# Chunked attention with a router behind it: the triangle inverse in 16-wide blocks and three rounds of products, the state's decay on VectorE, transfers and preparation in written order

## The chip, the cores and the metric

The kernel runs on one core of a Trainium2 chip. The metric is device time in microseconds (us), from the start to the end of one execution. Engines are named as in the profile: PE (TensorE), DVE (VectorE), ACT (ScalarE), POOL (GpSimd), SP (SyncE, which only issues transfers here).

## The reference

An attention with a state of 40 x 40 for each of 4 x 8 heads runs over 768 steps; its output, as 3072 rows of 320, goes through a mixture of 8 experts, two for each row.

```
for t in range(S):
    y[:, :, t] = np.einsum('bhd,bhde->bhe', rt, state)
    Sa = np.einsum('bhde,bhe->bhd', state, at)
    state_decay = state * wt[:, :, None, :] - np.einsum('bhd,bhe->bhde', Sa, bt)
    state = state_decay + np.einsum('bhd,bhe->bhde', vt, kt)
...
logits = x @ w_gate
noisy_logits = logits + np.log1p(np.exp(x @ w_noise)) * noise
# the two largest of 8 per row, softmax over the two
out[mask] += top2_w[mask, k, None] * (np.maximum(x[mask] @ w1[e], 0.0) @ w2[e])
```

## The kernel before

The 768 steps are done in chunks of 64. Within a chunk the recurrence is a triangular system, so that the kernel inverts a unit lower triangular 64 x 64 matrix for each head and does the rest with products. Two halves of the batch alternate (p = 0, 1), and two chunks (c = 0, 1) make a group g of 6: the work is a chain of 24 **units**, n = 4g + 2c + p, each one chunk of one half with 16 heads. The state `Sst[p]` goes from unit n to unit n + 2.

A unit issues on PE, in this order: `pkb` (UY<-P,kbt: the output of the unit before), `state` (pd and WS<-Sst,A), `rows` of the unit before (pg), `umm` (WS<-w,dT and UY<-dT,w: the product with the inverse), `akv` of the next unit (WS<-Vz,ak), `zmm` (UY<-dd,lo), `sumin` (WS<-Sst,idf: copies the state into the accumulator), `spmm` (WS<-vu,kbt), `dmm` (pD<-dd,Z), `rnmm`, `rmm`, and preparation for a later group: transposes (`quad`, ptr<-idf,KB) and scores (`score`, sc<-A,KB). ACT and DVE copy and scale between these; the first of it is ACT's copy w<-WS, which ends `state`. I count a unit from one such copy to the next.

Preparation of a group, per half: loads (raww, A, KB), a scan and `newton` on DVE, logarithm and exponential on ACT, the products `mula` and `mulk` (A<-A,Gx and KB<-KB,NH, 104x1024) on POOL, then scores. `prepS` copies the scores to `lt` and `lo` on ACT, and `lt` and the like go to DRAM (`scr`), from where `Solve` takes them as X, 128 lines of a 32 x 32 block. `Solve.step` makes the inverse of the 32-wide diagonal blocks in 30 pairs of multiply and add on X and Tt (30 to 240 elements a line); the table `SLV` says which pairs go to POOL and which to DVE, and in which slot of which unit. `done` writes X to DRAM, has ACT transpose it (Xn), and writes that. `fetchB` reads both back in 10 transfers for each unit (dd, dT), and `zmm` and `dmm` make the corner that joins the two 32-wide blocks of a chunk.

The class `Eng` (L397) makes each instruction on PE, DVE, ACT and POOL follow the one written before it on the same engine, and each waits there for its data. SP's order is left to the scheduler. The slots ('ld', 'p0', 'f1', 'p1', 'f2', 'f3', 'a1', 'qa', 'a2', 'qb', 'sc') are places in a unit's code where preparation is put by `ev`.

The router is `logits` for each unit (lg<-pg on DVE) and `route` after units 7, 15, 19, 21 and 23 (8, 8, 4, 2 and 2 tiles of 128 rows), which runs whole inside `finish` of the next unit: two dozen small instructions on DVE and ACT, products on PE (pr<-cnt,tri), then positions. `scatter` sends 4 indirect transfers a unit, or all that are left (ls<-ent, one for 128 entries, on POOL). The weights of the first expert (w1r, w2r) are loaded and split in two 16-bit parts by ACT and DVE (w1h, w1l, w2h, w2l) as soon as the scheduler places them, which is while the last units run. After unit 24's `finish` the eight experts run, to the end.

Of the kernel before, what the change touches and what calls it, by code (L numbers as in the profile page):

```python
# [17 lines left out]
R=104  # L18
# [27 lines left out]
class Moe:  # L46
    def __init__(s,nc,tc,ctx,aps):
        s.nc,s.tc=nc,tc
        s.wgn_d,s.nz_d,s.w1_d,s.w2_d,s.out_d=aps
        ec=ctx.enter_context  # L50
        s.kp=ec(tc.tile_pool(name="mk",bufs=1))
        s.rp=ec(tc.tile_pool(name="mr",bufs=MRB))
        s.dp=ec(tc.tile_pool(name="md",bufs=1,space=DRAM))
        s.scat=[]; s.half=0; s.parts=PARTS; s.cap=CAP; s.rts=list(RTS); s.todo=[]
        s.consts()
# [48 lines left out]
    def logits(s,n,xt,pl,ps,tag):  # L104
# [18 lines left out]
    def route(s,n0,T,ps,tag,bufs):  # L123
# [29 lines left out]
        if n0+T>=NA: s.scatter(len(s.todo))  # L153
    def scatter(s,n,after=()):
# [9 lines left out]
    def gate(s,lg,nzt,T,w0,w1):  # L164
# [249 lines left out]
class Solve:  # L414
    def __init__(s,a,g,scr):
        s.a,s.g,s.j,s.l=a,g,0,{}
        s.X=a.tmp.tile([128,32,32],F32,name="X"); s.T=a.tmp.tile([128,240],F32,name="Tt")
        s.fl=s.X.rearrange("p a b->p (a b)")
        s.xd=a.nc.sync.dma_start(s.fl,scr.rearrange("k p b x n->(k p b x) n"))
    def step(s,eng,n=1):  # L420
        X,T=s.X,s.T
        for _ in range(n):
            j=s.j; s.j+=1
            if j>30: return
            if j==0:
                s.a.nc.gpsimd.affine_select(out=X,in_=X,pattern=[[-1,32],[1,32]],base=0,channel_multiplier=0,compare_op=ALU.is_gt,fill=0.0)
                s.a.nc.gpsimd.memset(s.fl[:,0:1024:33],1.0)
            else:
                m=31-j; t=T[:,:j*m].rearrange("p (k i)->p k i",i=m)
                eng.tensor_tensor(t,X[:,j:j+1,j+1:].to_broadcast([128,j,m]),X[:,0:j,j:j+1].to_broadcast([128,j,m]),op=ALU.mult)  # L430
                s.l=eng.tensor_tensor(X[:,0:j,j+1:],X[:,0:j,j+1:],t,op=ALU.add)
    def done(s,eng):
        nc,a=s.a.nc,s.a
        s.step(eng,31)
        scr2=a.dr.tile([2,2,2,CG*8,1024],F32,name="scr2"); scr3=a.dr.tile([2,2,CG*8,1024],F32,name="scr3")
        nc.sync.dma_start(scr2.rearrange("k p b x n->(k p b x) n"),s.fl)
        Xn=a.inp.tile([64,32,32],F32,name="Xn",bufs=1)
        nc.scalar.activation(Xn,s.X[0:64].rearrange("p j t->p t j"),AF.Copy)
        nc.sync.dma_start(scr3.rearrange("p b x n->(p b x) n"),Xn.rearrange("p a b->p (a b)"))
        return scr2,scr3  # L440

class Att:
    def __init__(s,nc,tc,ctx,aps):
        s.nc,s.tc,s.aps=nc,tc,aps
        ec=ctx.enter_context
        s.inp=ec(tc.tile_pool(name="inp",bufs=1))
        s.tmp=ec(tc.tile_pool(name="tmp",bufs=1))
        o=sorted(range(SAB),key=lambda i:(i-2*NG)%SAB); s.sab={i:ec(tc.tile_pool(name=f"sab{i}",bufs=1)) for i in o}
        s.stk=ec(tc.tile_pool(name="stk",bufs=1))
# [8 lines left out]
        s.Z=s.UY[:,:,256:384].rearrange("p b (i t)->p b i t",t=32)  # L458
        s.consts()
    def consts(s):  # L460
# [4 lines left out]
        s.KB=[t([128,NS,2,64],F32,name=f"KB{i}") for i in range(2)]  # L465
        s.A=[t([128,NS,64],F32,name=f"A{i}") for i in range(SAB)]
# [10 lines left out]
        s.dT=[t([128,2,4,64],F32,name=f"dT{i}") for i in range(2)]  # L477
        s.Z2=t([128,2,4,64],F32,name="Z2")
# [13 lines left out]
    def burst(s,f):  # L492
        for g in f: i=g()
        return i
# [43 lines left out]
    def prepS(s,G,scr):  # L538
        nc=s.nc; sp,p=G['sp'],G['p']
        lt=s.tmp.tile([128,CG*2*4*32],F32,name="lt"); lo=sp.tile([128,32+CG*2*4*32],F32,name="lo")  # L540
        nc.gpsimd.memset(lo[:,0:32],0.0)
        G['lo']=lo; v=lambda z: z.rearrange("p (c q i t)->p c q i t",c=CG,q=2,i=4)
        pp=s.score(G,1)
        for z,t0 in ((lt,0),(lo[:,32:],32)): s.act(v(z).rearrange("p c q i t->p q c i t"),pp[:,:,:,t0:t0+32].rearrange("p q (c i) t->p q c i t",c=CG))
        for i in range(4):
            b,k=divmod(i,2)
            s.sl=nc.sync.dma_start(scr[k,p,b].rearrange("x (j t)->j x t",j=32),(lt,lo[:,32:])[k][32*i:32*i+32].rearrange("p (x t)->p x t",t=32))
    def prepK(s,G):
        ak=G['ak']=s.stk.tile([128,2,CG*4,64],F32,name="ak",bufs=AKB)
# [15 lines left out]
    def fetchA(s,o):  # L565
        nc=s.nc; p,cc=o['p'],o['cc']
        vu=o['vu']=s.stk.tile([128,2,2,4,40],F32,name="vu",bufs=VB)
        nc.sync.dma_start(vu[0:64].rearrange("p b q i e->p b (q i e)"),s.aps[1][p,cc].rearrange("(b s) x->s b x",b=2))
        rv=s.RV[o['n']%2]; nc.sync.dma_start(rv[0:R].rearrange("p x h t->p (x h t)"),s.aps[2][p,cc])
        o['r'],o['v']=rv[:,0],rv[:,1]  # L570
    def fetchB(s,o,S2):
        nc=s.nc; c,p=o['c'],o['p']; scr2,scr3=S2
        d=o['dT']=s.dT[o['n']%2]; dd=o['dd']=s.stk.tile([128,2,4,32],F32,name="dd",bufs=2)
        f=lambda z,q: z.rearrange("(c q i) (j t)->c q j i t",c=CG,q=2,j=32)[c,q]
        for b in range(2): nc.sync.dma_start(dd[64*b:64*b+32].rearrange("p q i t->p (q i) t"),scr3[p,b].rearrange("(c x) (j t)->c j x t",c=CG,j=32)[c])
        for q in range(2):
# [324 lines left out]
```

## Time and profile before

| | us |
|---|---|
| time, median of 3 runs | 1067.43 (1060.68 to 1069.38) |
| the profiled execution's own time | 1061.36 |
| its span in the trace | 1059.7 |
| up to the first unit's copy w<-WS | 93.4 |
| the 24 units, first to last such copy | 529.8 |
| last unit, last route, gather, experts | 436.5 |

The span is what the trace covers; 1.7 us of the execution lie outside it. In a row of the trace's timeline stand start, duration, engine, line, operation, output<-inputs with shape, how many instructions are merged, and in brackets the engine's idle time before them with the instruction that ended it ("issue" is none that the profile shows). Line 403 is the ordering wrapper, through which most instructions pass, so that they are told apart by tile names.

### The profile page before, as it was taken

How to read it: one execution, taken by the hardware profiler on the slowest of the kernel's cores; microseconds unless marked ns; L12 is line 12 of the kernel's file. 1: busy time of each engine (PE TensorE's matmuls, PEld its weight loads, DVE VectorE, ACT ScalarE, POOL GpSimd, SP SyncE). 2: the span in 40 equal slices, each digit the busy share in tenths (PEclk: the TensorE clock that was granted, in tenths of full speed). 3: DMA queues.
4: the chain of work that ended last, by engine and by line, in shares of the span. 5: the costliest groups of instructions: out<-in, count | busy, mean ns of one | idle time of the engine just before them, and what ended most of it. 6: DMA issues, size and time to landing. Idle time of an engine off the chain costs nothing. (4 is left out here: it accounts for less than half of the span.)

```text
span 1059.7 us, 29111 instructions
## 1 busy us (share of the span) xinstructions
PE 778.2 (73%) x12693; PEld 585.9 (55%) x12693; DVE 505.8 (48%) x1030; ACT 323.6 (31%) x654; POOL 370.8 (35%) x430
## 2 busy tenths in 40 slices
PE   1226555488658888668476661899999999999995
PEld 1114444477547777547365551475756666675663
DVE  8186364345446365513422207347556566555231
ACT  2024313133314234202221212245354434434231
POOL 8026330542464362352003101534334352531403
PEclk9967967659859789956665755899999999999998
DMA  8654733445637554512833523335434362621303
GB/s 193 162 96 91 157 77 85 102 103 140 134 83 148 136 129 120 138 23 76 231 112 93 139 58 124 82 58 166 92 100 99 94 156 53 173 25 17 38 10 38
DMA packets 187294, 110.00 MB, mean 104 GB/s; under 512 B 144818, under 2 KB 175414, under 8 KB 187078
## 3 DMA queue, kind: packets, MB, share of 16 engines
q1 hardware_dynamic: 174997, 90.90, 34.7%
q0 software_dynamic: 12160, 17.15, 9.2%
q8 instruction: 102, 1.67, 0.7%
q14 instruction: 35, 0.28, 0.1%
HBM read 81.73 MB, written 29.67 MB: 105 GB/s over the span
## 5 line engine op out<-in xcount | busy, mean ns | idle before, releaser
L303 POOL DMA_INDIRECT out_dram<-y,le x48 | 79.9, 1665 | 198.0 <-ACT y L297 196.4
L282 DVE SCALAR_TENSOR_TENSOR hl<-ph,hh 128x320 f16<-128x320 f32 (+1 forms) x128 | 74.1, 589 | 77.0 <-ACT hh L281 74.3
L281 ACT ACTIVATE hh<-ph 128x320 f16<-128x320 f32 (+1 forms) x128 | 65.9, 517 | 131.1 <-PE ph L280 109.9
L280 PEld LDWEIGHTS <-w1h 128*128 128x128 f16 x768 | 74.9, 99 | 54.7 <-issue 2.7
L294 PEld LDWEIGHTS <-hh 128*128 128x128 f16 (+1 forms) x1024 | 84.3, 101 | 35.0 <-issue 2.9
L403 PE MATMUL sc<-A,KB 64*64 64x64 f32 x1536 | 40.1, 275 | 79.6 <-ACT lo L403 21.6
L403 PEld LDWEIGHTS sc<-A,KB 64*64 64x64 f32 x1536 | 36.2, 184 | 85.0 <-issue 33.3
L403 POOL TENSOR_TENSOR KB<-KB,NH 104x1024 f32<-104x1024 f32 x20 | 51.0, 2570 | 69.0 <-PE pD L403 21.0
L294 PE MATMUL po<-w2h,hh 128*128 128x320 f16 (+1 forms) x512 | 73.2, 284 | 0.0
L403 DVE TENSOR_TENSOR Tt<-X 128x234 f32<-128x234 f32 (+14 forms) x128 | 52.5, 410 | 42.9 <-POOL X L403 39.7
L249 POOL DMA_INDIRECT xr<-xd,le x56 | 53.2, 950 | 50.9 <-issue 41.5
L294 PE MATMUL po<-w2h,hl 128*128 128x320 f16 (+1 forms) x512 | 68.6, 283 | 0.0
L294 PE MATMUL po<-w2l,hh 128*128 128x320 f16 (+1 forms) x512 | 67.9, 282 | 0.0
L280 PE MATMUL ph<-xh,w1h 128*128 128x512 f16 (+1 forms) x256 | 67.5, 347 | 0.5 <-DVE hl L282 0.5
L280 PE MATMUL ph<-xl,w1h 128*128 128x512 f16 (+1 forms) x256 | 66.5, 341 | 0.0
L280 PE MATMUL ph<-xh,w1l 128*128 128x512 f16 (+1 forms) x256 | 66.4, 341 | 0.0
L403 PE MATMUL UY<-P,kbt 128*64 128x64 f32 x768 | 36.7, 262 | 34.3 <-DVE P L403 29.2
L403 DVE TENSOR_TENSOR P<-sc,mk 128x512 f32<-128x512 f32 x48 | 30.8, 684 | 50.7 <-PE sc L403 50.7
L403 POOL DMA_INDIRECT ls<-ent,po x48 | 48.8, 1016 | 17.4 <-issue 12.2
L297 ACT ACTIVATE y<-po,le 128x320 f32<-128x320 f32 (+1 forms) x56 | 28.3, 505 | 84.6 <-PE po L294 84.5
L403 PEld LDWEIGHTS UY<-P,kbt 128*64 128x64 f32 x768 | 32.5, 172 | 37.6 <-DVE P L403 30.6
L403 PE MATMUL pD<-dd,Z 32*64 32x32 f32 x768 | 37.6, 245 | 20.9 <-ACT Z L403 12.1
(214 smaller groups left out, 1613.0 us busy)
## 6 DMA issues: line engine op xcount, KB each, us to landing
w2r<-in_w_dram SPq DMA_DIRECT2D x8, 1280.0 KB
KB<-in_fm_dram SPq DMA_DIRECT2D x24, 416.0 KB
RV<-in_rv_dram SPq DMA_DIRECT2D x24, 416.0 KB
w1r<-in_w_dram SPq DMA_DIRECT2D x8, 1024.0 KB
raww<-in_fm_dram SPq DMA_DIRECT2D x12, 422.5 KB
A<-in_fm_dram SPq DMA_DIRECT2D x12, 416.0 KB
w1r<-in_w_dram SPq DMA_DIRECT2D x16, 256.0 KB
vu<-in_vt_dram SPq DMA_DIRECT2D x24, 160.0 KB
```

The lines of the kernel that those rows point to most:

```text
L249: for k in range(c,c+a): nc.gpsimd.indirect_dma_start(out=x[:p,k],out_offset=None,in_=s.xd[w],in_offset=OFFS(ap=li[:p,k,0:1],axis=0))
L280: for i,(a,b) in enumerate(mm): nc.tensor.matmul(ph[:,:n],a,b,start=i==0,stop=i==7)
L281: nc.scalar.activation(hh[:,f],ph[:,:n],AF.Relu)
L282: nc.vector.scalar_tensor_tensor(hl[:,f],ph[:,:n],0.0,hh[:,f],op0=ALU.max,op1=ALU.subtract)
L294: for j in range(c): nc.tensor.matmul(po[p*j:p*j+p,:d],h[:,f,r],w[:,f,d*j:d*j+d],start=k==0,stop=k==23)
L297: nc.scalar.activation(y[:,:d],po[:,:d],AF.Copy,scale=w_[:,ii:ii+1])
L303: st=nc.gpsimd.indirect_dma_start(out=o_,out_offset=OFFS(ap=ix,axis=0),in_=yv,in_offset=None,compute_op=ALU.add)
L403: i=f(*a,**kw)
```

## The change

- **Inverse**: `Solve` works on 16-wide diagonal blocks, two for each line of 32, in 14 pairs of 28 to 112 elements. Pairs of all groups but the first are on POOL, in slot f1 of unit 4g-3, and `done` is in slot f2 of unit 4g-2. The first group's are on DVE, ahead of the units.
- **Products**: with N the score matrix without its diagonal blocks and D the block inverses, `mm1` forms M = DN and its transpose, `mm2` forms G = I + M² and H (with D), and `mm3` forms GH, which is added to D; `zmm` and `dmm` go. DVE adds the identities and D, ACT copies MT and H. D and its transpose are fetched into XD (every second unit, both halves) and XDT (each unit), each a single buffer.
- **State**: `sumin` goes; DVE adds `Sp` to `Sst` and multiplies by `ge`, in two instructions where there was one.
- **Order**: after the first part SP is put in written order too. The transfers scr<-lt are kept back in `late` and issued at the next unit's start (`flush`). Each unit but the last five now has the same kind of preparation, two quads and one score.
- **Router**: `route` is a generator that moves one step at each of six calls of `adv()` in a unit; `acc` moves from POOL to DVE.
- Tiles are fixed (`own`), no more taken from pools.

```diff
 class Solve:
     def step(s,eng,n=1):
-            if j>30: return
+            if j>14: return
...
-                m=31-j; t=T[:,:j*m].rearrange("p (k i)->p k i",i=m)
-                eng.tensor_tensor(t,X[:,j:j+1,j+1:].to_broadcast([128,j,m]),X[:,0:j,j:j+1].to_broadcast([128,j,m]),op=ALU.mult)
-                s.l=eng.tensor_tensor(X[:,0:j,j+1:],X[:,0:j,j+1:],t,op=ALU.add)
+                m=15-j; sh=[128,2,j,m]; t=s.T[:,:2*j*m].rearrange("p (a k i)->p a k i",a=2,i=m)
+                eng.tensor_tensor(t,V[:,:,j:j+1,j+1:].to_broadcast(sh),V[:,:,0:j,j:j+1].to_broadcast(sh),op=ALU.mult)
+                s.l=eng.tensor_tensor(V[:,:,0:j,j+1:],V[:,:,0:j,j+1:],t,op=ALU.add)
     def done(s,eng):
-        Xn=a.inp.tile([64,32,32],F32,name="Xn",bufs=1)
-        nc.scalar.activation(Xn,s.X[0:64].rearrange("p j t->p t j"),AF.Copy)
+        nc.scalar.activation(a.Xn,s.fl.rearrange("p (j t)->p t j",t=32),AF.Copy)
...
-    def fetchB(s,o,S2):
+    def fetchD(s,o,S2):
         for q in range(2):
+            for k in range(2): s.nc.sync.dma_start(s.XD[64*q+32*k:64*q+32*k+32].rearrange("p i b u t->p (i b u) t")[:,:,32*k:32*k+32],S2[0][k,o['c'],q].rearrange("i b p (j t)->j (i b p) t",j=32))
+    def fetchT(s,o,S2):
+        for b in range(2):
+            for k in range(2): s.nc.sync.dma_start(s.XDT[64*b+32*k:64*b+32*k+32,:,32*k:32*k+32],S2[1][k,o['c']][:,:,b,o['p']].rearrange("q i (t j)->t (q i) j",t=32))
...
+    def mm1(s,o,G):
+        for z in range(2):
+            for h,b in QB():
+                q,i=h%2,h//2; r=slice(64*b,64*b+64); x=D[r,4*q+i],N[r,q,4*c+i]
+                s.mm(pp[64*q:64*q+64,b,z,i],x[z],x[1-z],start=True,stop=True)
+        s.nc.vector.tensor_tensor(s.M1,pp[:,:,0],s.Ir.rearrange("p (o u) t->p o u t",u=1).to_broadcast([128,2,4,64]),op=ALU.add)
+        s.act(s.MT,pp[:,:,1])
...
-    def sumin(s,o): s.mm(s.Sp,s.idf,s.Sst[o['p']][...,0:40],start=True,stop=False)
...
-        s.nc.vector.tensor_tensor(s.Sst[o['p']][0:R,:,:,0:40],s.Sp[0:R],o['ge'].to_broadcast([R,4,2,40]),op=ALU.mult)
+        S=s.Sst[o['p']][0:R,:,:,0:40]
+        s.nc.vector.tensor_tensor(S,s.Sp[0:R],S,op=ALU.add); s.nc.vector.tensor_tensor(S,S,o['ge'].to_broadcast([R,4,2,40]),op=ALU.mult)
...
         for n in range(N+1):
-            if n<N: do(n,'ld'); fV(n+2)
+            s.flush(); do(n,'ld'); fV(n+2); do(n,'ld2')
             if r: s.pkb(r,Gof(n-1))
...
+            if x: s.mm1(x,Gof(n+1))
+            adv()
             if r: finish(r,n-1)
-            do(n,'f1')
+            adv()
             s.umm(o)
...
-            if n!=2: fB(n+2)
-            if n+1<N: s.akv(O[n+1],Gof(n+1)); s.zmm(O[n+1],Gof(n+1))
-            if not last: s.sumin(o); s.spmm(o,G)
+            if x: s.mm2(x); s.akv(x,Gof(n+1))
+            adv()
+            if not last: s.spmm(o,G)
+            fA(n+2)
             do(n,'f2')
-            if n+1<N: s.dmm(O[n+1])
-            if not first: s.rnmm(o)
             s.rmm(o)
-            fA(n+2)
-            do(n,'f3')
+            adv()
+            if x: s.mm3(x); fT(n+2); fD(n+2)
             do(n,'a1'); do(n,'qa',"pA"); do(n,'a2'); do(n,'qb',"pB"); do(n,'sc')
+            adv()
+            if not first: s.rnmm(o)
+            fR(n+2)
```

**First place: DVE in unit 3.** Numbers behind a name tell the buffers of one name apart. Before, the pairs of group 2's inverse (Tt, X) stand between the state (Sst) and the mask P, which `pkb` needs:

```order
L403 TENSOR_TENSOR Sst_138<-WS,ge 104x8x40
L403 TENSOR_TENSOR Tt<-X 128x130
L403 TENSOR_TENSOR X<-X,Tt 128x5x26
L403 TENSOR_TENSOR Tt<-X 128x150
L403 TENSOR_TENSOR X<-X,Tt 128x6x25
L403 TENSOR_TENSOR P<-sc,mk 128x512 x2
```

Of the change, from one scan (Gx, ge) to the unit's last instruction there, No:

```order
L422 SCALAR_TENSOR_TENSOR Gx_173<-raww_73,d_246 104x1024
L422 TENSOR_TENSOR ge_193<-Gx_173,raww_73 104x16
L422 TENSOR_TENSOR Ms<-sc,Ir 128x512
L422 TENSOR_REDUCE lg<-pg 128x16
L422 TENSOR_TENSOR Gs<-sc,Ir 128x512
L422 TENSOR_TENSOR Sst_263<-WS,Sst_263 104x8x40
L422 TENSOR_TENSOR Sst_263<-Sst_263,ge_197 104x8x40
L422 TENSOR_TENSOR P<-sc,mk 128x512 x2
L422 TENSOR_TENSOR dT<-UY,XD 128x512
L422 TENSOR_TENSOR No_105<-sc,mB 128x1024
```

The pairs that waited for POOL's have left DVE; Ms, Gs, dT, the second Sst and No have come.

**Second place: PE in unit 8, where the first route falls.** Before, pr stands right behind pg, ahead of `umm`:

```order
L403 MATMUL ptr<-idf,KB_117 128x128 x8
L403 MATMUL sc<-A_119,KB_117 64x64 x32
L403 MATMUL UY<-P,kbt 64x64 x16
L403 MATMUL pd<-idf,Sst_137 128x128 x4
L403 MATMUL WS<-Sst_137,A_122 64x40 x16
L403 MATMUL pg<-IW,yT 128x120 x4
L403 LDWEIGHTS tri
L403 MATMUL pr<-cnt,tri 128x64
```

Of the change, from `pkb` to `spmm`, where a whole unit's new order is seen:

```order
L422 MATMUL UY<-P,kbt_213 64x64 x16
L422 MATMUL pd<-idf,Sst_263 128x128 x4
L422 MATMUL WS<-Sst_263,A_165 64x40 x16
L422 MATMUL sc<-No_105,XDT 64x64 x16
L422 MATMUL sc<-XDT,No_105 64x64 x16
L422 MATMUL pg<-IW,yT 128x120 x4
L422 MATMUL WS<-w_274,dT 64x40 x16
L422 MATMUL UY<-dT,w_274 64x64 x16
L422 MATMUL sc<-MT,Ms 64x64 x16
L422 MATMUL sc<-XD,MT 64x64 x16
L422 MATMUL WS<-Vz_266,ak_125 64x80 x8
L422 MATMUL WS<-vu_270,kbt_217 40x40 x16
```

and, further on in the same unit, behind `rmm`:

```order
L422 MATMUL UY<-Hs,Gs 64x64 x16
L422 MATMUL ptr<-idf,KB_101 128x128 x8
L422 MATMUL sc<-A_169,KB_97 64x64 x32
L422 LDWEIGHTS tri
L422 MATMUL pr<-cnt,tri 128x64
```

`mm1` stands between `state` and pg, `mm2` between `umm` and `akv`, and pr has moved to the unit's end, behind the score.

**Third place: DVE in units 18 and 19, where the first two experts' weights come.** Before, expert 0's split stands in unit 18 between lg and P:

```order
L403 TENSOR_REDUCE lg<-pg 128x16
L205 TENSOR_REDUCE mx<-w1r 128x1
L223 SCALAR_TENSOR_TENSOR w1l<-w1r,w1h 128x1024 x2
L224 SCALAR_TENSOR_TENSOR w1h<-w1r,w1h 64x1024
L208 TENSOR_REDUCE yc<-w1l 128x1
L403 TENSOR_TENSOR Sst_137<-WS,ge 104x8x40
L208 TENSOR_REDUCE yc<-w1h 64x1
L205 TENSOR_REDUCE mx<-w2r 128x1
L233 SCALAR_TENSOR_TENSOR w2l<-w2r,w2h 128x640 x4
L205 TENSOR_REDUCE mx<-w1r 128x1
L403 TENSOR_TENSOR P<-sc,mk 128x512 x2
```

Of the change, from unit 18's last copies to unit 19's Gs (ak is group 5's):

```order
L224 TENSOR_REDUCE mx<-w2r 128x1
L242 SCALAR_TENSOR_TENSOR w1l<-w1r,w1h 128x1024 x2
L243 SCALAR_TENSOR_TENSOR w1h<-w1r,w1h 64x1024
L252 SCALAR_TENSOR_TENSOR w2l<-w2r,w2h 128x640
L227 TENSOR_REDUCE yc<-w1l 128x1
L252 SCALAR_TENSOR_TENSOR w2l<-w2r,w2h 128x640 x2
L422 TENSOR_TENSOR yT<-UY,Gx_185 104x2x4x64
L227 TENSOR_REDUCE yc<-w1h 64x1
L252 SCALAR_TENSOR_TENSOR w2l<-w2r,w2h 128x640
L224 TENSOR_REDUCE mx<-w1r 128x1
L422 TENSOR_TENSOR Ms<-sc,Ir 128x512
L422 TENSOR_REDUCE lg<-pg 128x16
```

The split now lies across the border of the two units, ahead of yT, and the second expert's first instruction (mx<-w1r) ahead of Ms; its mx<-w2r is the next row, ahead of Gs.

## Rows read from the trace of the kernel before

**Rows 1.** The page's first part, one engine: busy time, share of the span, instructions.

```profile
PE 778.2 (73%) x12693; PEld 585.9 (55%) x12693; DVE 505.8 (48%) x1030; ACT 323.6 (31%) x654; POOL 370.8 (35%) x430
```

**Rows 2.** Busy time by stretch, cut at the copies w<-WS of units 0, 5, 8, 16, 20 and 23. [...]

```profile
0.00:93.40 93.40, 23.42 (x440) 17.61 (x440) 56.96 (x99) 19.68 (x31) 37.74 (x82) 0.86 0.64 138
93.40:235.40 142.00, 86.40 (x2219) 74.08 (x2219) 69.56 (x112) 36.99 (x79) 52.70 (x62) 0.72 0.48 107
235.40:286.80 51.40, 40.08 (x1267) 35.01 (x1268) 26.62 (x56) 17.80 (x40) 17.02 (x24) 0.93 0.58 133
286.80:441.30 154.50, 121.46 (x3386) 104.85 (x3386) 80.00 (x187) 49.43 (x111) 74.49 (x92) 0.83 0.53 121
441.30:551.40 110.10, 68.50 (x1418) 58.65 (x1418) 36.19 (x104) 22.97 (x50) 22.47 (x33) 0.63 0.43 117
551.40:623.20 71.80, 45.96 (x1025) 39.63 (x1025) 17.33 (x82) 12.21 (x35) 13.29 (x20) 0.64 0.36 97
```

**Rows 3.** The same view of unit 14 alone.

```profile
411.50:426.50 15.00, 12.70 (x424) 11.17 (x423) 5.11 (x13) 6.10 (x12) 2.19 (x4) 1.00 0.45 121
```

**Rows 4.** The timeline of PE in unit 14, the rows of `akv`, `zmm`, `sumin`, `dmm`, the quads and the score.

```profile
415.50 0.77 PE L403 MATMUL WS<-Vz,ak 128*64 128x80 f32 x16 [1.82 <-ACT vu L403]
416.20 0.67 PE L403 MATMUL UY<-dd,lo 32*64 32x32 f32 x32
416.80 0.81 PE L403 MATMUL WS<-Sst,idf 128*128 128x320 f32 x2
...
418.27 1.12 PE L403 MATMUL pD<-dd,Z 32*64 32x32 f32 x32
...
420.88 1.09 PE L403 MATMUL ptr<-idf,KB 128*128 128x128 f32 x8
422.46 1.16 PE L403 MATMUL sc<-A,KB 64*64 64x64 f32 x64 [0.48 <-DVE Tt L403]
```

**Rows 5.** The timeline of DVE in unit 14, the state and the mask P.

```profile
418.46 0.49 DVE L403 TENSOR_TENSOR Sst<-WS,ge 104x320 f32<-104x320 f32 x1 [3.66 <-PE WS L403]
421.02 1.29 DVE L403 TENSOR_TENSOR P<-sc,mk 128x512 f32<-128x512 f32 x2 [2.07 <-PE sc L403]
```

**Rows 6.** The timeline ahead of the units: first and last DVE instruction of the first group's inverse, and ACT's first w<-WS.

```profile
54.25 0.19 DVE L403 TENSOR_TENSOR Tt<-X 128x30 f32<-128x30 f32 x1 [1.51 <-POOL X L403]
...
76.03 0.21 DVE L403 TENSOR_TENSOR X<-X,Tt 128x30 f32<-128x30 f32 x1
...
93.43 0.45 ACT L403 ACTIVATE w<-WS 128x320 f32<-128x320 f32 x1
```

**Rows 7.** The timeline of units 2 and 3: what waited for an inverse.

```profile
167.13 1.96 ACT L403 ACTIVATE Xn<-X 64x1024 f32<-64x1024 f32 x1 [13.53 <-DVE X L403]
...
169.72 1.54 PE L403 MATMUL ptr<-idf,KB 128*128 128x128 f32 x6 [11.87 <-ACT kbt L403]
...
200.25 1.01 PE L403 MATMUL UY<-P,kbt 128*64 128x64 f32 x14 [11.73 <-DVE P L403]
```

**Rows 8.** The costliest groups of POOL's instructions, shapes apart: count | busy us, mean ns | idle time before them.

```profile
L403 POOL TENSOR_TENSOR KB<-KB,NH 104x1024 f32<-104x1024 f32 x20 | 51.0, 2570 | 69.0 <-PE pD L403 21.0 <-PE UY L403 19.7 <-DMA KB<-in_fm_dram 17.4
...
L403 POOL TENSOR_SCALAR_AFFINE_SELECT X<-X 128x1024 f32<-128x1024 f32 x6 | 7.6, 1262 | 101.0 <-DMA X<-scr 56.1 <-DMA KB<-in_fm_dram 32.9 <-ACT dT L403 12.1
...
L403 POOL TENSOR_TENSOR X<-X,Tt 128x108 f32<-128x108 f32 x5 | 2.0, 393 | 0.4
...
L403 POOL TENSOR_TENSOR X<-X,Tt 128x30 f32<-128x30 f32 x2 | 0.5, 236 | 0.2
```

**Rows 9.** The timeline of unit 14: SP's issue of a group's load of X, and the first POOL instruction on it.

```profile
416.88 0.34 SPq L419 DMA_DIRECT2D X<-scr  x1
...
420.59 1.27 POOL L403 TENSOR_SCALAR_AFFINE_SELECT X<-X 128x1024 f32<-128x1024 f32 x1 [12.74 <-DMA X<-scr]
```

**Rows 10.** The timeline of PE at the route in unit 8.

```profile
295.90 0.21 PE L403 MATMUL pr<-cnt,tri 128*128 128x64 f16 x1 [8.06 <-DVE cnt L403]
```

**Rows 11.** Unit 16's scatters: the first and the last of 13 in POOL's timeline, and a stretch of 6 us within them (columns as in the second group).

```profile
453.22 1.02 POOL L403 DMA_INDIRECT ls<-ent,po  x1 [0.49 <-DVE po L403]
...
468.44 0.96 POOL L403 DMA_INDIRECT ls<-ent,po  x1 [0.30 <-issue]
...
459.00:465.00 6.00, 2.07 (x17) 1.57 (x17) 0.00 (x0) 0.38 (x1) 4.47 (x6) 0.50 0.03 2
```

**Rows 12.** The timeline of unit 18: the first expert's weights on ACT, SP's issue of w2r, and PE.

```profile
513.04 2.00 ACT L222 ACTIVATE w1h<-w1r 128x1024 f16<-128x1024 f32 x2 [8.69 <-DMA w1r<-in_w_dram]
...
514.15 0.40 SPq L216 DMA_DIRECT2D w2r<-in_w_dram  x1
...
516.72 1.92 PE L403 MATMUL pD<-dd,Z 32*64 32x32 f32 x32 [10.17 <-ACT Z L403]
...
520.85 2.62 ACT L232 ACTIVATE w2h<-w2r 128x640 f16<-128x640 f32 x4 [4.18 <-DMA w2r<-in_w_dram]
```

**Rows 13.** The timeline of unit 1: one POOL product and the DVE instructions beside and behind it.

```profile
134.33 2.34 POOL L403 TENSOR_TENSOR A<-A,Gx 104x1024 f32<-104x1024 f32 x1
134.40 2.47 DVE L403 TENSOR_TENSOR Tt<-X 128x184 f32<-128x184 f32 x1 [12.60 <-POOL X L403]
136.91 0.35 DVE L403 TENSOR_TENSOR X<-X,Tt 128x184 f32<-128x184 f32 x1
```

More of the change, by code (lines that the diff above doesn't have):

```diff
@@ L53, in __init__ @@
         s.dp=ec(tc.tile_pool(name="md",bufs=1,space=DRAM))
[L54 removed]
+        s.scat=[]; s.steps=[]; s.half=0; s.parts=PARTS; s.cap=CAP; s.rts=list(RTS); s.todo=[]
         s.consts()
@@ L122, in turn, with advance, route @@
         s.half=1
-    def route(s,n0,T,ps,tag,bufs):
+    def advance(s,all=False):
+        while s.steps:
+            if next(s.steps[0],None) is None: s.steps.pop(0)
+            elif not all: return
+            if not all: return
+    def route(s,n0,T,lg,ps,tag,bufs):
         nc=s.nc
         w=s.ent[:,n0:n0+T,:,2]
-        lg=s.lg[:,0:T]
-        oh=s.gate(lg,s.nz[:,n0:n0+T],T,w[:,:,0],w[:,:,1])
+        lg=lg[:,0:T]
+        nc.vector.tensor_tensor(s.acc[:,0:T],s.acc[:,0:T],lg,op=ALU.add)
+        oh=yield from s.gate_(lg,s.nz[:,n0:n0+T],T,w[:,:,0],w[:,:,1])
         nc.vector.tensor_scalar(w,w,YS,None,op0=ALU.mult)
-        nc.gpsimd.tensor_tensor(s.acc[:,0:T],s.acc[:,0:T],lg,op=ALU.add)
         r=lambda name,sh=(8,),dt=F32: s.rp.tile([128,RT,*sh],dt,name=name)[:,0:T]
         cnt=r("cnt",dt=F16); nc.vector.tensor_tensor(cnt,oh[:,:,0],oh[:,:,1],op=ALU.add)
+        yield 1
         pr=ps.tile([128,T,8],F32,name="pr",tag=tag,bufs=bufs)
@@ L163, in scatter, with gate, gate_ @@
         s.todo=s.todo[n:]
-    def gate(s,lg,nzt,T,w0,w1):
+    def gate(s,*a):
+        g=s.gate_(*a)
+        while True:
+            try: next(g)
+            except StopIteration as e: return e.value
+    def gate_(s,lg,nzt,T,w0,w1):
         nc=s.nc
@@ L490, in consts, with flush @@
         s.dm=t([128,320],F16,name="dm"); nc.vector.memset(s.dm,0.0)
-    def burst(s,f):
-        for g in f: i=g()
-        return i
+    def flush(s):
+        for f in s.late: s.sl=f()
+        s.late=[]
     def mm(s,*a,**k): s.nc.tensor.matmul(*a,skip_group_check=True,**k)
@@ L733, in do @@
+        for g in range(1,NG): prep(g)
         def do(n,slot,*a):
@@ L740, in run @@
             o=O[n] if n<N else None; r=O[n-1] if n else None
-            if n<N: do(n,'ld'); fV(n+2)
+            s.flush(); do(n,'ld'); fV(n+2); do(n,'ld2')
             if r: s.pkb(r,Gof(n-1))
-            if n==N: finish(r,n-1); break
-            G=Gof(n); first=o['cc']==0; last=o['cc']==NG*CG-1; w1=s.w1[n%2]
+            if n==N:
+                if m is not None: m.advance(True)
+                finish(r,n-1)
+                if m is not None: m.advance(True)
+                break
+            G=Gof(n); first=o['cc']==0; last=o['cc']==NG*CG-1; w1=s.w1[n%2]; x=O[n+1] if n+1<N else None
+            do(n,'f1'); adv()
             s.unit(o,G)
```

235 lines of the change are left out of this document (121 added, 114 removed).

## The prediction

> **What bounds the kernel now.** I read the page's first part first: PE is busy for 778.2 of 1059.7 us, more than any other engine [rows 1]. That average mixes two programs, so I cut the span at the starts of units [rows 2]. From unit 23 to the end (436.5 us, the experts) the change touches almost nothing. The 530 us of units are my subject, and with them the 93.4 us ahead.
>
> What should a unit take? Unit 14 took 15.0 us at a granted clock of 1.00 with PE busy for 12.70 [rows 3]; the idle 2.3 us are mostly one gap of 1.82 us, where `akv` waits for ACT's copy vu [rows 4]. 23 such units would be 345 us; from first to last start they took 529.8. So about 185 us are stalls and the slow clock that goes with them. In the first five units PE is busy for 86.4 of 142.0 us at a mean clock of 0.72; in units 16 to 19 for 68.5 of 110.1 at 0.63 [rows 2].
>
> Then I asked for the stalls themselves. They are of four kinds.
> (1) The inverse. Its pairs alternate between POOL and DVE, and both engines keep written order. In unit 2 ACT idles 13.53 us ahead of Xn, and PE, whose quads need ACT's copies, 11.87; in unit 3 P stands behind pairs that wait for POOL, and PE idles 11.73 [rows 7].
> (2) The route. Written whole ahead of `umm`, it holds PE for 8.06 us in unit 8 [rows 10].
> (3) The scatters. Thirteen in a row take POOL from 453.22 to 469.4. In 6 us of that PE ran 17 matmuls, at half clock, while the DMA engines were 3% busy [rows 11]. This is no dependency; the trace names no releaser.
> (4) The first weights: ACT idles 8.69 us for w1r with Z queued behind, and PE 10.17 [rows 12].
>
> **The change part by part.** *A steady unit.* PE loses `zmm`, `sumin` and `dmm` (0.67 + 0.81 + 1.12 = 2.60) [rows 4]. `mm1` and `mm2` are each as many 64x64 products as a score, 1.16 [rows 4]; `mm3` is half that, 0.58: 2.90 in all. PE's work is 12.7 - 2.6 + 2.9 = 13.0 us. `mm2` is written ahead of `akv`, where the 1.82 us gap was. Its own inputs (Ms from DVE, MT from ACT) have pg and `umm` as cover. What is left is idle time that I can't read off: at least none (13.0), at most the 2.3 of before (15.3). I take 1.5, since three rounds put three new crossings between engines into each unit: **14.5**. Without quads and score (1.09 + 1.16 [rows 4]) I take 12.5 for units 19 to 23.
>
> DVE gains Ms, Gs, dT (each half of a P pair's 1.29, so 0.65), a second Sst (0.49) and No (twice 0.65) [rows 5], some 3 us on average, and loses its pairs. With 5.1 us of work in unit 14 [rows 3] it has room. ACT's three copies replace Z, dT and one of two lt/lo copies: even.
>
> *The inverse* falls from 60 instructions of 30 to 240 elements to 28 of 28 to 112. On POOL a pair's half costs 0.24 us at 30 and 0.39 at 108 elements [rows 8]; at 0.33 each and 0.08 idle (0.4 for 5 of the group of 108), 28 are 11.5 us, with affine_select (1.26) and memsets 13. It stands in one place, nobody's work between. The chain of a group is: scores' transfers at the start of unit 4g-3, X issued some 6 us in, landed 3.7 us later (416.88 to 420.59 [rows 9]), 13 us of pairs, Xn at about 8 us into unit 4g-2, its ACT copy 2, write, XDT read back (two more trips of 2 to 4 us), so 17 us, while `mm1` of unit 4g is written 17.6 us after that unit's start. It fits by a hair; I book 3 us a group.
>
> *Ahead of the units*: the first inverse ran on DVE from 54.25 to 76.24, 22 us for 60 instructions, 0.37 each [rows 6]. 28 small ones at 0.29 are 8: **-14**. Three rounds instead of two add between 0 and 8 (each a product group, a copy and two handovers, about 2 to 4); I take 4. Net **-10**, the first w<-WS at 83.4.
>
> *Units 0 to 4* [rows 2]: 142.0 before. Kind (1) is gone, preparation is spread evenly: 5 x 14.5, and 8 for loads that come late and group 1's inverse, which has only two units: 80, **-62**.
>
> *Units 5 to 7*: 51.4 before; 3 x 14.5 + 3 = 46.5: **-5**.
>
> *Units 8 to 15*: 154.5 before. The route moves in single steps at `adv()`, so its 8 us hold is spread; I keep 3. The scatters stay. They are declared independent of each other, the order shows 13 in one piece again, and nothing in the change slows POOL's issue. By 18 us of burst in which PE did less than 5 us of full-speed work, a burst of 13 costs 13. 8 x 14.5 + 13 + 3 + two inverses 6 = 138: **-16.5**.
>
> *Units 16 to 19*: 110.1 before. Two clean units 29, one inverse and one route 6; unit 18 with the 16 scatters of the second route 14.5 + 17; unit 19 with the weights 12.5 + 22: 101, **-9**. The 22: ACT and DVE still stand in written order behind w1r and w2r, with single buffers. The second expert's w1r can't start before the first's split ends (about 2.0 + 1.1 on ACT, then DVE), needs about 5, and Ms is queued behind its mx; Gs behind that of w2r, which took 6.7 us from issue to ACT (514.15 to 520.85 [rows 12]). Before it was 10.17 [rows 12] and a shorter one.
>
> *Units 20 to 22*: 71.8 before; 3 x 12.5 + scatters 9 and 4 + 3 = 53.5: **-18**. *The rest*, 436.5 less 1.7 outside: the last route still runs whole, so 0.
>
> Sum: -10 - 62 - 5 - 16.5 - 9 - 18 = **-120.5**. From this execution's 1061.4 that is 941. The median of the runs shown, 1067.43, lies 6 above it, so I write **945**.
>
> [...] In unit 1 a DVE instruction of two SBUF inputs (Tt) took 2.47 us beside POOL's A<-A,Gx of 2.34; the next, of the same size, 0.35 [rows 13]. The new second Sst instruction has both inputs in SBUF, where the old one had PSUM for one, and POOL's products of 2.57 us [rows 8] now run in most units. [...]
>
> **The rivals.** *B, the bursts and weights don't cost what they did.* With POOL's stream now holding pairs and products, and steps of the route at other times, the burst may fall where PE has little left, or weights may land under cover. For: they are not bound to the units by any data. Against: a burst slowed PE wherever it fell, without a releaser [rows 11]. 13 + 17 + 9 of bursts and 15 of weights less: 890.
>
> *C, the inverse is late once per group.* My margin is 0.6 us. If late, ACT stands behind Xn for some 8 us with w<-WS queued, and the clock falls as in rows 2 (0.63 to 0.72 where stalls stand), 6 more: 14 for 5 groups, 70, less the 15 booked: 1000. For: 13.53 us before [rows 7] had just this cause. Against: the pairs are half, and DVE is out of them.
>
> [...]
>
> *E, no net gain*: the units are limited by something that my cut doesn't show (transfers: the DMA share is 0.45 at 15 us a unit [rows 3] and would rise only to about 0.5), and stalls return one by one: 1065.
>
> [...]
>
> **How the numbers follow.** A (my sum, 905 to 985) 0.57; B 0.15; C 0.13; D 0.06; E 0.04; F 0.05. A's own width: the steady unit at 13.0 or 15.3 moves 20 units by -30 or +16, the first five units are known to 15, the weights to 15. The range takes in B's and C's middles and D: 885 to 1010, about 0.84. A difference under 1% can't be told from none with runs that spread by 0.8%. All of A to D are faster by far more: faster 0.91, same 0.04, slower 0.05.
>
> **What would show it.** The first w<-WS near 83; units without incident of 14.5 us at clock 1.00 with PE busy for about 13.0; no gap of over 3 us on PE ahead of sc<-No,XDT or behind ACT's Xn in units 4g-2 to 4g; no idle time ahead of P for Tt or X; pr<-cnt without an 8 us gap. Thirteen and sixteen ls<-ent in a row with "issue" gaps on PE beside them, and one long wait for w1r or w2r around unit 19. I am wrong if POOL's pairs take clearly over 13 us, if ACT's Xn comes later than 10 us into its unit, or if PE waits for XDT in ordinary units.

## The result, and the profile after

The changed kernel takes 1002.53 us (median of 4 runs, 991.67 to 1014.79) against 1068.41; the ratio is 0.933 (95% interval 0.922 to 0.944). That is 6.7% less by the ratio: faster and in the range, but 58 us above the forecast of 945. Two of these four executions take 1.5% or more above the fastest; the medians hold such executions, the ratios leave them out. The profiled execution took 991.67 us, its span 990.0.

The same stages as in [rows 2], cut at the same units (busy time by stretch; the columns of both: the stretch and its length in us, busy time of PE, PEld, DVE, ACT and POOL with their instructions, PE's granted clock as a share of its full speed, the DMA engines' busy share, GB/s):

```profile
0.00:94.10 94.10, 30.81 (x553) 24.12 (x557) 45.94 (x75) 20.97 (x31) 37.59 (x83) 0.84 0.63 129
94.10:182.30 88.20, 69.18 (x2486) 62.61 (x2484) 44.44 (x63) 31.12 (x62) 32.18 (x39) 0.90 0.69 140
182.30:240.00 57.70, 43.98 (x1564) 40.01 (x1558) 28.25 (x38) 20.62 (x41) 22.66 (x35) 0.91 0.67 145
240.00:401.60 161.60, 122.04 (x4153) 108.86 (x4148) 82.29 (x151) 53.78 (x111) 72.15 (x98) 0.86 0.66 139
401.60:502.00 100.40, 66.85 (x2015) 58.88 (x2009) 46.78 (x105) 26.76 (x56) 33.20 (x57) 0.75 0.55 143
502.00:557.00 55.00, 40.30 (x1302) 35.40 (x1292) 20.76 (x72) 12.74 (x34) 8.51 (x12) 0.81 0.49 130
557.00:990.00 433.00, 388.01 (x2946) 253.25 (x2946) 223.29 (x416) 164.48 (x311) 157.35 (x124) 0.95 0.37 85
```

| stage | forecast | measured |
|---|---|---|
| ahead of the units | -10 | +0.7 |
| units 0 to 4 | -62 | -53.8 |
| units 5 to 7 | -5 | +6.3 |
| units 8 to 15 | -16.5 | +7.1 |
| units 16 to 19 | -9 | -9.7 |
| units 20 to 22 | -18 | -16.8 |
| the rest | 0 | -3.5 |
| sum | -120.5 | -69.7 |

Three rows carry most of the miss, 45.6 of 50.8 us: the time ahead of the units, units 5 to 7 and units 8 to 15. All three became longer, the last although its hold of 8.06 us at the route [rows 10] is gone. What does PE wait for now? The view of waits, PE alone, first to last w<-WS (columns: what waited and for whom; us in total, times, longest), of before:

```profile
PE pr L403 <- DVE cnt L403: 28.1, 4, 8.2
PE UY L403 <- DVE P L403: 21.3, 7, 11.7
PE ptr L403 <- ACT kbt L403: 19.4, 8, 11.9
PE sc L403 <- DVE ak L403: 16.8, 2, 15.4
PE UY L403 <- issue: 14.3, 19, 2.6
...
PE WS L403 <- issue: 10.4, 12, 1.1
...
PE pD L403 <- issue: 8.8, 16, 1.2
```

and of the changed kernel:

```profile
PE UY L422 <- issue: 37.4, 36, 2.6
PE sc L422 <- issue: 34.1, 35, 3.9
PE WS L422 <- issue: 14.3, 9, 4.5
PE sc L422 <- ACT Hs L422: 7.6, 8, 4.2
...
PE sc L422 <- DMA XDT<-scr: 2.5, 5, 0.7
PE pr L422 <- DVE cnt L422: 2.3, 2, 2.1
```

The waits for P, kbt, ak and cnt, 86 us in the upper block, are gone or small. "Issue", where nothing shown releases PE, grew from 33.5 to 85.8 us in the three rows shown of each; a part of it stands beside scatters.

Where do these gaps stand? In unit 7 PE stops for 4.52 us in the middle of 32 equal products of the same tiles, 29 of them done (PE's timeline, SP's, and then the DMA view of two stretches in that gap: packets and share by queue):

```profile
226.11 0.74 PE L422 MATMUL WS<-vu,kbt 128*40 128x40 f32 x29
231.37 0.33 PE L422 MATMUL WS<-vu,kbt 128*40 128x40 f32 x3 [4.52 <-issue]
```

```profile
221.06 0.39 SPq L422 DMA_DIRECT2D A<-in_fm_dram  x1
221.49 5.74 SPq L422 DMA_DIRECT2D KB<-in_fm_dram  x2
227.28 3.95 SPq L422 DMA_DIRECT2D Vz<-in_vt_dram  x2
```

```profile
q1 hardware_dynamic: 956, 0.24, 104.5%
...
q1 hardware_dynamic: 891, 0.23, 102.1%
q8 instruction: 1, 0.02, 5.4%
```

From 226.9 to 228.5 the packets of data take 104.5% of the 16 DMA engines' time, and there is none of the queue called instruction; from 228.5 to 230 there is one, and PE goes on at 231.37. The page counts that queue over the whole span:

```profile
q8 instruction: 119, 1.95, 0.9%
```

PE and PEld have 2 x 14953 rows there: 251 for each packet of 16.4 KB. The gaps fit that. Between the gap that ends at 205.50 and the one that ends at 209.85, and between the latter and the one that ends at 214.71, PE ran (busy time by stretch):

```profile
205.40:209.50 4.10, 3.02 (x127) 2.70 (x127) 2.08 (x4) 3.49 (x6) 3.71 (x7) 1.00 1.05 186
209.50:214.50 5.00, 3.28 (x127) 2.91 (x128) 2.31 (x4) 1.49 (x3) 4.96 (x3) 1.00 1.04 310
```

254 and 255 instructions, about one packet's share; I call that many a block. What the trace shows, packet by packet: 39 of PE's idle times without releaser, 57.9 us together, end 1.2 to 1.85 us behind the end of one of the 90 packets of that queue in the units (before: 10 idle times, 10.8 us). I read this as PE standing where its next block of code hasn't arrived. Of four of them, in us:

| gap ends | its length | packet starts | packet takes | from its end to the gap's |
|---|---|---|---|---|
| 157.45 | 3.83 | 154.52 | 1.43 | 1.50 |
| 187.44 | 2.04 | 184.90 | 1.18 | 1.36 |
| 231.37 | 4.52 | 228.58 | 1.29 | 1.50 |
| 393.01 | 3.91 | 390.04 | 1.47 | 1.51 |

What differs is when the packet starts. The one for unit 7's gap starts 4.49 us after PE entered the block before (at 224.09); in the 17 places where two such gaps follow each other it is 1.0 to 4.5 us, and from the end of one gap to that of the next at least 3.49 us, where a block is about 3.2 us of PE's work (13.26 us for 2 x 532 rows in unit 13, shown further down).

Numbers below called **block gaps** are PE's idle times of over 0.1 us without releaser, first to last w<-WS, summed from the trace, without those beside a scatter: 14.8 us before, 57.0 after. They say little in small steps: counted by packets as above, six runs that leave the units' loads as they are (e3, e4, e5, e8, e9, e11) have 53 to 64 us.

### The profile page after: what moved, and what is told of

Same layout as the page of the kernel before. It is cut to its first block, busy times and chain, and to the rows that moved or that the text cites. A ratio compares the mean times of both kernels' runs of the same rounds, so it can differ in the third digit from the quotient of the medians.

```text
span 990.0 us, 33278 instructions
## 1 busy us (share of the span) xinstructions
PE 761.2 (77%) x14953; PEld 583.1 (59%) x14953; DVE 491.7 (50%) x915; ACT 330.5 (33%) x642; POOL 363.6 (37%) x448
## 5 line engine op out<-in xcount | busy, mean ns | idle before, releaser
L422 POOL TENSOR_TENSOR KB<-KB,NH 104x1024 f32<-104x1024 f32 x20 | 47.3, 2389 | 69.3 <-DVE NH L422 36.7
L422 PEld LDWEIGHTS sc<-A,KB 64*64 64x64 f32 x1536 | 33.8, 169 | 59.2 <-issue 31.6
L422 ACT ACTIVATE kbt<-ptr 128x320 f32<-128x320 f32 x48 | 20.9, 436 | 109.1 <-PE ptr L422 109.0
L316 ACT ACTIVATE y<-po,le 128x320 f32<-128x320 f32 (+1 forms) x56 | 28.3, 505 | 84.6 <-PE po L313 84.5
L422 PE MATMUL sc<-RV 64*64 64x64 f32 x768 | 38.2, 247 | 21.8 <-issue 13.8
L422 POOL TENSOR_SCALAR_AFFINE_SELECT X<-X 128x1024 f32<-128x1024 f32 x6 | 7.9, 1311 | 125.2 <-DMA X<-scr 125.2
L422 POOL DMA_INDIRECT ls<-ent,po x48 | 46.7, 972 | 17.6 <-issue 12.9
L227 DVE TENSOR_REDUCE yc<-y 128x1 f32<-128x320 f32 (+1 forms) x56 | 25.4, 460 | 55.1 <-ACT y L316 54.6
```

The source lines that it names most:

```text
L227: s.nc.vector.tensor_reduce(s.yc[q:128,s.ny:s.ny+1],a,axis=AX.X,op=ALU.add); s.ny+=1
L316: nc.scalar.activation(y[:,:d],po[:,:d],AF.Copy,scale=w_[:,ii:ii+1])
L422: i=f(*a,**kw)
```

## The experiments

Ratios are to the kernel before, with their 95% intervals; the changed kernel's is 0.933 (0.922 to 0.944).

**Lighter traffic (e1_light).** `fetchV` and `fetchR` issue their transfers only for units 0 and 1 (the line of `fetchR`):

```diff
...
+        if o['n']<2: nc.sync.dma_start(rv[0:R].rearrange("p x h t->p (x h t)"),s.aps[2][p,cc])
...
```

> The changed kernel, but from unit 2 on the loads of RV and Vz are left out (their tiles keep what units 0 and 1 loaded, so the outputs are others). 2 to 3 us less of DMA engine time in each unit's 12. Theory T1, that PE's instruction blocks (a gap without releaser each 254 records) come late because they queue behind data: the block gaps fall from 57 us to 35 or less, and the time by 20 to 35 us against the changed kernel. Rival T2, that blocks come late because PE now needs more of them in less time, whatever the traffic: gaps 50 to 60 us, time within 8 us. Rival T3, that the gaps only stand in for another wait: gaps fall, but the time stays.

Measured: 968.17 us, 0.909 (0.904 to 0.914); block gaps 44.4 us.

**Heavier traffic (e2_heavy).** One more load a unit, into a spare tile:

```diff
...
+        if o['n']>1: nc.sync.dma_start(s.XT[0:R].rearrange("p x h t->p (x h t)"),s.aps[2][p,cc])
...
```

> The changed kernel with one more load of 416 KB in each unit from 2 on, into a tile that nobody reads, issued right behind RV's. 1.5 us more DMA engine time a unit. T1: block gaps grow from 57 to 70 to 90 us, the time by 12 to 35 us against the changed kernel. T2: gaps as before, time within 8 us. A second way to a longer time is that XDT or vu land later; then the gaps on PE name XDT or ACT vu instead of no releaser.

Measured: 1011.76 us, 0.949 (0.944 to 0.955); block gaps 65.3 us. By the ratios the one took some 25 us less than the changed kernel and the other 18 more, as T1 has it, with little more than half of the least expected size in the gaps (by packets 44.7 and 76.2 us, outside the 53 to 64 above); T2 and T3 alone fall. In the lighter run the first to last w<-WS took 28.3 us less, more than the 12.6 of the gaps: 12.2 more stand in PE's busy time (342.4 to 330.2), with its mean clock up from 0.84 to 0.89.

**Fewer, larger pieces (e10_kbpack).** KB's halves are interleaved in the input and come in one transfer (the line of the load):

```diff
...
-        o=XW+X+X*(1-z); s.nc.sync.dma_start(G['kb'][0:R,:,z],...)
+        if z: s.nc.sync.dma_start(G['kb'][0:R].rearrange("p a z t->p (a z t)"),s.aps[0][G['p'],G['g']][:,XW+X:XW+3*X])
```

> The changed kernel with KB's two halves laid side by side in the input, so that they come in one transfer of 104 pieces of 8 KB instead of two of 1664 pieces of 256 bytes; same bytes, same outputs. By the packets' times in the changed kernel's trace (27 ns for the small, 280 ns for 8 KB) some 1.9 us less DMA engine time a unit. T1 with the slope of the lighter and heavier run: block gaps from 57 to about 46 us, time 12 to 25 us less, for the clock comes back with the gaps. T2 (pace alone): within 5 us.

Measured: 1018.65 us (6 runs, 1001.23 to 1025.71; no ratio), block gaps 73.3 us. Its two fastest, 1001.23 and 1002.1, lie some 8 us above those of the changed kernel, 991.67 and 996.6, where 12 to 25 less were expected. The DMA share fell from 0.62 to 0.58, and still the gap of unit 7 grew from 4.52 to 6.47:

```profile
226.81 0.29 PE L423 MATMUL WS<-vu,kbt 128*40 128x40 f32 x6
233.57 0.36 PE L423 MATMUL WS<-vu,kbt 128*40 128x40 f32 x4 [6.47 <-issue]
```

That gap's packet starts 6.5 us after PE entered the block before, against 4.49. So my form of T1 falls, in which DMA time by itself is what a block waits for. The saving was smaller than booked, too: the 8 KB pieces took 578 ns each on average in this run, not 280, so that some 0.9 us of DMA engine time a unit went, not 1.9. KB, 832 KB in all, is now issued in 1.3 us instead of 5.74. What the three runs share is bulk ahead of the block: less of it, smaller block gaps (44.4 us against 57.0); more, or more at once, larger ones (65.3 and 73.3). That gaps end 1.2 to 1.85 us behind a packet is shown (39 times); that PE waits for it, and that it starts late because it stands behind data, is argued from this, not shown.

**Written order of SP undone (e4_sp_free)**: the line `nc.sync=Eng(nc0.sync,s.tc)` is left out.

> The changed kernel with the transfers of the units left to the scheduler again instead of in written order; all else as changed. If written order is what packs transfers into bursts ahead of the instruction blocks: block gaps fall to 30 us or less and the time by 15 us or more. If the traffic alone does it: gaps 45 to 65 us, time within 10 us. If written order is a gain by itself (transfers that are needed first come first): slower by over 10 us, with waits for XDT or RV on PE.

Measured: 1026.60 us, 0.963 (0.959 to 0.968); block gaps 56.6 us. Written order isn't what makes the gaps (57.0 us with it), and it is worth some 3%. In unit 3 PE waits for XDT, whose way leads over scr<-Xn. ACT's Xn ends at 147.21; its transfer is issued 7.5 us later, behind loads of KB, raww, A and Vz (SP's and PE's timeline):

```profile
148.36 0.92 SPq L533 DMA_DIRECT2D KB<-in_fm_dram  x1
149.39 2.91 SPq L528 DMA_DIRECT2D raww<-in_fm_dram  x1
...
154.70 0.57 SPq L459 DMA_DIRECT2D scr<-Xn  x1
...
162.51 1.82 SPq L599 DMA_DIRECT2D XDT<-scr  x4
...
164.88 0.44 PE L422 MATMUL sc<-No,XDT 64*64 64x64 f32 x2 [14.85 <-DMA XDT<-scr]
```

**The state's decay undone (e8_sumin)**: `sumin` is back ahead of `spmm`, and DVE has one instruction again.

> The changed kernel with one part undone: sumin is back on PE (0.8 us a unit) and the state's decay is one DVE instruction again. If PE's own work sets the units: 14 to 20 us longer. If the blocks' arrival does: under 8 us longer. [...]

Measured: 998.93 us, 0.936 (0.926 to 0.946): no difference that can be told. Its two fastest runs (983.92 and 993.59) lie below the changed kernel's, so that 0.8 us of PE's work a unit shows nothing here of the 14 to 20 us that it would cost if PE's own work set the units.

**The route undone (e9_route)**: `adv` calls `m.advance(True)`.

> The changed kernel with one part undone: each call of adv runs the whole rest of a route, so that a route stands ahead of umm again. By the rows of before (8.06, 8.22, 6.3 and 5.5 us of hold for four routes, and the slow clock with them): 20 to 32 us longer. If the spread route's instructions cost as much elsewhere (DVE's queue, the scatters at another time): under 10 us.

Measured: 1043.28 us, 0.978 (0.966 to 0.989): by the ratios some 48 us longer than the changed kernel, by the two traces 44, more than expected. In unit 8 PE waits 12.11 us for cnt, where it was 8.06 [rows 10]:

```profile
250.37 0.21 PE L422 MATMUL pr<-cnt,tri 128*128 128x64 f16 x1 [12.11 <-DVE cnt L422]
```

**The scatters spread (e5_spread)**: the line `after=()` in `scatter` goes, so that all four of a unit follow its rows. **Left out (e13_noscat)**: `if j<16: continue`.

> The changed kernel with the first route's scatters four to a unit (each now ordered behind that unit's rows) instead of 13 in a row; the second route's 16 stay in a row. If each scatter holds PE for about a microsecond wherever it stands: time within 8 us of the changed kernel. If only a row of them does (transfers and PE both stand still in it): unit 10's 18 us of excess fall away, some 12 to 18 us less.

> The changed kernel without the 32 scatters of the first two routes (their lists stay unwritten, so the outputs are others; all else runs). If each scatter holds PE for about a microsecond: units 10 and 18 fall from 34.8 and 38.6 to 16 to 20 us, and the time by 30 to 42 us. If PE only waits there for what it would wait for anyway: under 15 us less.

Spread: 991.86 us, 0.931 (0.927 to 0.935), the same: units 9 to 14 took 119.5 us together instead of 122.3. Without them the whole takes 10063 us, because rows that no list holds send the program into its slow general path; but its units can be read: unit 10 takes 18.1 us instead of 34.8, as expected; unit 18 29.2 instead of 38.6, not the expected 16 to 20, and there PE now waits 7.46 us for ak. So the first 13 scatters cost 16.7 us, in a row or spread, and the 16 of unit 18 cost 9.4.

**The time ahead of the units.** e3_prolog writes group 1's newton and KB products ahead of `mm1`; e11_prolog2 puts the newton, the first KB product and the first scores there, with KB's second load behind XD:

```diff
...
+        nh(1,0); bm(1,0); L(1,0)
         nc.sync=Eng(nc0.sync,s.tc)
...
+        fT(0); fD(0); k_(1,0); s.mm1(O[0],Gof(0)); fT(1); km(1,0); s.mm2(O[0]); s.mm3(O[0])
...
```

> The changed kernel with group 1's first newton and its products on KB written ahead of the first mm1 instead of behind mm3. If the first w<-WS (94.1 us) waits for that preparation and not for the inverse (dT at 84.4): the first w<-WS comes at 86 to 89, and the time falls by 5 to 8 us. If something else is late there: within 3 us.

> The changed kernel with group 1's first newton, its first product on KB and its first scores ahead of mm1, and KB's second half loaded behind the first XDT and XD, so that no load stands ahead of the inverse's way through DRAM. If preparation in front of the first w<-WS is what took the 10 us booked ahead of the units: first w<-WS at 85 to 88 instead of 94.1, time 5 to 9 us less. If it is again something on SP's queue: first w<-WS over 91 and time within 3 us.

The first w<-WS came at 92.9 and 90.8 instead of 94.1, later than the expected 86 to 89 and 85 to 88; 997.98 us, 0.938 (0.930 to 0.946), and 1004.56 us, 0.942 (0.935 to 0.948). In the first the loads of KB, now ahead, held SP, and XDT was issued at 78.30 instead of 72.31. Neither time can be told from the changed kernel's; e12_all, below, brings the first w<-WS down.

**Vz without transfers (e6_vz)**: ACT copies it from vu.

```diff
...
+        for b in range(2): s.act(vz[64*b:64*b+64,:,b],o['vu'][0:64,b].rearrange("p q i e->p (q i) e"))
...
```

> The changed kernel with Vz made by two ACT copies from vu (0.43 us each, written behind sD, where ACT idles 2.3 us) instead of two transfers of 512 pieces of 160 bytes a unit; the outputs are the reference's. 1.0 us less DMA engine time a unit, 2 to 4 us less of SP's queue. By the slope that the lighter and the heavier run gave (0.22 to 0.25 us of block gap for each us of DMA engine time) the gaps fall from 57 to about 51; with SP's queue the time falls by 5 to 12 us. If T2 (pace alone): within 4 us, or ACT's copies make it longer.

Measured: 985.70 us (974.19 to 997.24; no ratio), block gaps 54.4 us. Without these small pieces the gaps are little smaller (57.0 with them). Its two fastest runs, 974.19 and 981.02, lie some 16 us below the changed kernel's, more than the 5 to 12 expected; where that comes from isn't shown.

**Together (e12_all).**

> The changed kernel with the edits of the runs on the prologue, Vz, KB and the first route's scatters together, and raww of the second half loaded one unit earlier; the outputs are the reference's. T1: some 3 us less DMA engine time in a unit's 12, so block gaps of 35 us or less, and the first w<-WS at 85 to 88: 30 to 45 us less than the changed kernel, about 960. T2: 8 to 15 us less.

Measured: 978.74 us, 0.919 (0.914 to 0.924), the fastest but for e1, which leaves loads out; the first w<-WS at 83.6, block gaps 50.6 us. By the ratios that is some 15 us less than the changed kernel. The two traces differ by 23: 10 ahead of the units and 14 in them, less 1 behind them. The expected 35 us or less of gaps did not come, and since e6 alone is nearly as fast (974.19 and 981.02 against 968.58 and 976.88 for the two fastest here), hardly anything that the other edits add is shown.

## Why the prediction was right, and where its sum failed

**Right.** The stalls of kinds (1) and (2) are gone: the pairs no longer alternate, and P and the quads wait for no inverse; the spread route holds PE for 2.3 us in all units together. The route's part and that of SP's order were undone by themselves and cost some 48 and 33 us, more than the whole gain together, so that parts don't add up here; the inverse's part rests on the waits of before and after, no run undoes it alone. PE's work came out: unit 13 has 13.26 us busy at full clock, 13.0 forecast:

```profile
345.40:360.80 15.40, 13.26 (x532) 11.89 (x528) 9.56 (x13) 6.61 (x15) 4.78 (x12) 1.00 0.59 131
```

**The step that failed** is the steady unit's last one: "What is left is idle time that I can't read off ... I take 1.5: 14.5". Units 1 to 9 and 11 to 17 take 18.5 us on average (295.3 for 16), 63 us more than 16 times 14.5. Of that, 26 us stood in the sum under other names (late loads 8, inverses 12, routes 6), so that 37 of the 50.8 us that it is short are missing here. Of the 18.5 us PE idles 3.8, not 1.5, and 3.1 of these are without releaser; it is busy for 14.6, for its granted clock, which I had at 1.00, is 0.84 over all units and below 1.00 in 11 of these 16 (unit 5: busy for 15.8 at 0.83; unit 13, above: 13.26 at 1.00). The cause of the idle time, as I read it, is the wait for code (39 idle times, 57.9 us, in all units together). I bounded the idle time by unit 14 of before; but that unit runs 424 products in 15.0 us [rows 3], while the new one has 532 to run in 13 and more transfers beside them. The trace of before held the sign: "issue" idle times away from scatters, up to 2.8 us long (at 368.65, unit 11), which I took for nothing. No rival of mine had it; E, the nearest, named transfers, but not what waits for them. That the range held is in part luck: the measured 1002.53 lies outside A's own 905 to 985, and the range reached that far only for C and D, whose mechanisms did not come.

**The time ahead of the units** failed in the second place: "Net -10, the first w<-WS at 83.4". The pairs did fall to 7.7 us and dT was there at 84.4. Then w<-WS waited until 94.06 behind ACT's copies for group 1, whose newton DVE ran only after dT: a chain that I hadn't followed (the timeline of DVE and ACT):

```profile
83.72 0.69 DVE L422 TENSOR_TENSOR dT<-UY,XD 128x512 f32<-128x512 f32 x1 [1.88 <-PE UY L422]
84.33 1.20 DVE L422 TENSOR_TENSOR NH<-Gx,raww 104x1008 f32<-104x1008 f32 x1
...
91.47 1.03 ACT L422 ACTIVATE lt<-sc 128x1024 f32<-128x1024 f32 x1 [9.00 <-PE sc L422]
...
93.73 0.44 ACT L422 ACTIVATE kbt<-ptr 128x320 f32<-128x320 f32 x1 [0.42 <-PE ptr L422]
94.06 0.43 ACT L422 ACTIVATE w<-WS 128x320 f32<-128x320 f32 x1
```

With that preparation ahead, and less on SP, it is 83.6 (e12_all, with other edits beside).

**Mis-sized terms.** Scatters: 13 and 17 booked, 16.7 and 9.4 measured. The weights: 22 booked for unit 19; it took 25.9 against 12.2 of unit 20, so 13.7. The route: 8 us a hold understated it, some 48 in all with its clock and its moved scatters. The inverse booked 3 us a group, but all waits for XDT are 2.5. That is so although two signs of being wrong came: POOL's affine_select and pairs take 13.7 to 15.6 us for 13, and Xn comes 11.1 and 10.2 us into units 2 and 14.

**Rivals.** C fell with these 2.5 us. D, at 990 in the range, has the second Sst instruction up to 2.1 us longer (2.57 [rows 8] less 0.49 [rows 5]) beside a product of POOL in each of 22 units. No run shows that; what the changed kernel shows is this, all 22 of them (duration in ns, least/median/most):

```profile
L422 DVE TENSOR_TENSOR Sst<-Sst,ge x22: 491/492/1549, 101.4 to 521.7; 104x320 f32<-104x320 f32 x22
```

The median is that of an undisturbed one (0.49 [rows 5]); one at most lost 1.06 us. B's part on scatters fell for the first 13, while the 16 of unit 18 cost 9.4 of the 17 booked; its part on weights was half right. F, slower at 0.05, has SP's written order hold up the way to XDT and the clock at half in every unit. No run shows either: XDT is late with SP's order undone (14.85 us in unit 3), not with it (2.5 us in all units), and the mean clock of the units is 0.84.

## What to carry to other kernels

When stalls are removed from an engine with thousands of short instructions, look at when its code comes: count instructions for each packet of the queue called instruction (251 here), look for idle times without releaser at that spacing (254 and 255), and see what transfers are issued ahead of them. An idle time that the profile puts down to nothing is a cost, and here it grew as the others went (33.5 to 85.8 us in the three rows shown of each). Lay it beside those packets before you explain it. Follow what stands ahead of a stage's first instruction on every engine, not only the chain that you shorten; and don't count on work cut from an engine whose idle times end behind such packets: here 0.8 us a unit showed nothing (ratios 0.933 without `sumin`, 0.936 with it).

## What the runs showed of the hardware that was not expected

- PE stopped for up to 4.52 us between two of 32 equal products. Of its idle times without releaser 39 end 1.2 to 1.85 us behind a 16.4 KB packet of the queue called instruction; between three of them in a row lie 254 and 255 instructions. With KB in larger pieces and one transfer ahead the stop of 4.52 us was 6.47 (e10_kbpack).
- Where two such stops follow each other (17 places), the packet of the second starts 1.0 to 4.5 us after the end of the first, and the two ends are at least 3.49 us apart.
- With 13 scatters on POOL a unit takes 16.7 us more than without them (34.8 and 18.1, e13_noscat), with no releaser shown on PE, while the DMA engines' share is 0.03 [rows 11], 0.19 (unit 10, 289 to 305 us) or 0.57 (unit 18, 448 to 468 us, beside the weights). What does that stays open.
- The slowing of [rows 13] goes the other way too: two of POOL's small steps in unit 9 (at 276.65 and 277.97) took 1.25 and 1.48 us beside DVE's newton, where their neighbours took 0.40 and 0.39.
- Open: how much of the block gaps is the pace of the code alone (3.49 us at least from border to border, for about 3.2 of PE's work) and what delays the packets that start later.
